# Clears and early weight tiles on another DMA queue, tables ahead of the loop, later tiles behind a gather

## The chip, the cores and the metric

The kernel runs on one core of a Trainium2 chip. Its engines are TensorE (PE, with its weight loads as PEld), VectorE (DVE), ScalarE (ACT), GpSimd (POOL) and SyncE (SP, which issues DMAs). All times are microseconds on the device; less is better. One execution was profiled; the times beside it are of executions without a profile.

## The reference

Causal block attention over 8 batches of 8 heads (576 positions, 64 wide, blocks of 64), then a mixture of 8 experts in which each token goes to its best expert and each expert keeps its 80 tokens with the highest gate:

```python
scores = scale * np.matmul(q, k.transpose(0, 1, 3, 2))
scores = np.where(block_i >= block_j, scores, -1000000000.0)
attn = np.exp(scores - np.max(scores, axis=-1, keepdims=True))
attn = attn / (np.sum(attn, axis=-1, keepdims=True) + 1e-09)
x = np.matmul(attn, v)                     # then (B * S, H * D) = (4608, 512)
...
logits = x @ w_gate                        # (4608, 8)
expert_idx = np.argmax(logits, axis=1)
gate_w = softmax(logits)[arange, expert_idx]
out = zeros((4608, 512))
for e in range(8):
    tok_idx = np.where(expert_idx == e)[0]         # the 80 with the highest gate_w of these
    h = np.maximum(x[tok_idx] @ w1[e], 0.0)        # w1[e]: 512 x 1024
    out[tok_idx] = gate_w[tok_idx, None] * (h @ w2[e])
```

Every row of `out` that no expert writes is zero.

## The kernel before, in words

**Attention.** 32 pairs of heads (4 pairs a batch) run through a software pipeline: turn `i` of the loop at the end of `tile_attn_moe` does, in an order written out in the table `TURN`, the load of pair `i+3` (`load`: four DMAs for q, four for k, into one of three buffers each, lines L392 before and L394 after), the transposes of pair `i+1` (`prep`, DVE, L406 / L409, the q one followed by a scale on POOL, L409 / L412), the scores, maxima and exponentials of pair `i` and the transposes and products with v of pair `i-1`. The Tile framework keeps this order on each engine. The loop starts at `i = -3`. SP issues all loads in order; DVE runs `prep` in order with the maxima of the scores, so a q that has not landed holds up DVE, and PE after it.

**Beside the loop.** Zeros are written to `out` by 18 DMAs of 512 KB (`clear`, L150), in most turns from 4 on, out of a tile `zero`. Three weight tiles of 2 MB (`weights`, L233 / L235; tiles 0 to 2 of 16, the list alternates between w1 and w2) are loaded in turns 8, 16 and 24: the "early tiles". After each batch its rows, their sums and the gate logits are made; `store` writes them to `xs` in DRAM. Tables that the selection uses are made by `constants` (POOL, in turn 3) and `constants2` (DVE and POOL, in turn 5). In `constants2` DVE's table `iota_c16` (L212) needs POOL's `iota_c` (L210), the last of a row of POOL instructions that starts with a copy (L198) of DVE's `sameE` (L195).

**Selection and experts.** After the last store the kernel picks the tokens of each expert (the indices `gi`), POOL gathers each expert's 80 rows from `xs` (L735 / L738, `fetches`), DVE divides them by their sums (`xn`, L824), PE transposes two experts' rows ahead and then multiplies by w1 and w2 (L835 / L840) expert by expert; POOL scatters the result to `out` (L872). The 13 later tiles are issued by SP: two after the last store, a third after `gi`, three more after the fourth gather (`fetches[HOLD]`), the rest one by one between the experts as buffers come free.

Of the kernel before, what the change touches and what calls it, by code (L numbers as in the profile page):

```python
# [18 lines left out]
P = 128  # L19
BLK = 64  # L20
NT = 5
FW0, FWA, FWC, FWB = 3, 3, 1, 2
# [56 lines left out]
def tile_attn_moe(ctx, tc, q, k, v, w_gate, w1, w2, capacity, out, xs=None, dbg=None):  # L79
    nc = tc.nc  # L80
# [41 lines left out]
    for i in range(4):  # L122
        r = slice(32 * i, 32 * i + 32)
# [18 lines left out]
    zero = pb.tile([P, 2 * DM], F32, name="zero")  # L142
    rows = 2 * P
    ov = out.rearrange("(n p r) d -> n p r d", p=P, r=2) if NTOK % rows == 0 else None
    nz = NTOK // rows

    def clear(i):
        if ov is not None:
            if 0 <= i < nz:
                nc.sync.dma_start(ov[i], zero.rearrange("p (r d) -> p r d", r=2))  # L150
        elif i == 0:
            for j in range(NTOK // BLK):
                nc.sync.dma_start(out[j * BLK:(j + 1) * BLK, :], zero[0:BLK, 0:DM])
# [39 lines left out]
    def constants2():  # L193

        nc.vector.tensor_reduce(sameE, ident.rearrange("p (e j) -> p e j", j=16), axis=AX.X, op=ALU.add)  # L195
        nc.gpsimd.memset(sameR3, 0.0)
        nc.vector.tensor_reduce(sameR, ident.rearrange("p (e j) -> p j e", j=16), axis=AX.X, op=ALU.add)
        nc.gpsimd.tensor_copy(same.rearrange("p (e j) -> p e j", j=16), sameE.unsqueeze(2).broadcast_to([P, E, 16]))  # L198
        nc.gpsimd.memset(ones, 1.0)
        nc.gpsimd.iota(iota_s, pattern=[[1, CHUNK]], base=0, channel_multiplier=0,  # L200
                       allow_small_or_imprecise_dtypes=True)
        nc.gpsimd.iota(iota_p, pattern=[[0, 1]], base=0, channel_multiplier=1, allow_small_or_imprecise_dtypes=True)

        nc.gpsimd.affine_select(out=before, in_=same, compare_op=ALU.is_gt, fill=0.0, base=0,
                                pattern=[[1, P]], channel_multiplier=-1)
        nc.gpsimd.affine_select(out=after, in_=same, compare_op=ALU.is_gt, fill=0.0, base=0,
                                pattern=[[-1, P]], channel_multiplier=1)
        nc.gpsimd.tensor_tensor(before1, before, ident, op=ALU.add)
        nc.gpsimd.tensor_tensor(after1, after, ident, op=ALU.add)
        nc.gpsimd.iota(iota_c, pattern=[[1, 16]], base=0, channel_multiplier=0,  # L210
                       allow_small_or_imprecise_dtypes=True)
        nc.vector.tensor_tensor(iota_c16, sameR, iota_c, op=ALU.mult)  # L212
        nc.vector.tensor_reduce(iota_r, iota_c16, axis=AX.X, op=ALU.add)

        nc.gpsimd.tensor_copy(cf, ci)
        nc.vector.scalar_tensor_tensor(cap, cf[:, 1:2], 4294967296.0, cf[:, 0:1], op0=ALU.mult, op1=ALU.add)
        nc.vector.tensor_tensor(caplt, iota_p, cap, op=ALU.is_lt)

    nw = 0
# [5 lines left out]
    def weights(n, after=None):  # L225

        nonlocal nw
        for _ in range(n):
            src, e = wlist[nw]
            w_ = wpools[nw % len(wpools)].tile([P, KP * F], F32, name="w")  # L230
            nw += 1
            wt_[src is w2, e] = w_ = w_.rearrange("p (a f) -> p a f", f=src.shape[2])
            load = nc.sync.dma_start(w_, src[e].rearrange("(a p) f -> p a f", p=P))  # L233
            if after is not None:
                tc.add_manual_dep(load.ins, after.name, mybir.DependencyInfo(  # L235
                    mybir.DependencyClass.Sync, mybir.DependencyReason.DATA))
# [136 lines left out]
    class Pair:  # L373
# [10 lines left out]
        def load(self):  # L384

            b, h0 = self.b, self.h0
            self.nat = [ld.tile([P, S // 32, 32], F32, name=f"ld{x}") for x in range(2)]
            for x in range(2):
                for h in range(2):
                    for i in range(2):  # L390
                        r = slice(h * D + 32 * i, h * D + 32 * i + 32)
                        nc.sync.dma_start(self.nat[x][r], (q, k)[x][b, h0 + h, :, 32 * i:32 * i + 32]  # L392
                                          .rearrange("(g r) d -> r g d", r=32))

        def load_v(self):
# [160 lines left out]
    def step():  # L556
        if todo:
            f, *args = todo.pop(0)
            f(*args)

    with tc.manual_schedule():
        warm(WARM[0], ps_m.tile([P, 512], F32, name="pm"))
        for i in range(-3, n + 2):
            if i == -1:
                nc.sync.dma_start(ci, capacity.bitcast(U32).partition_broadcast(P))
                for h in range(2):
                    nc.sync.dma_start(wgd[h * D:(h + 1) * D, :, h * E:(h + 1) * E], wg_v[h])

            if i >= 4 and (i % 2 or i % 8 == 4) and i < n:
                clear(cleared)  # L570
                cleared += 1
            if i == 3:
                constants()
            if i == 5:
                constants2()
            if i in range(n // 4, n // 4 + 8 * FW0, 8):
                weights(1)
            for d, what, *args in TURN:
                if what == "step":
                    step()  # L580
                elif 0 <= i + d < n and not (what == "flip" and i + d >= n - NP):
                    getattr(pairs[i + d], what)(*args)
            if n - NP <= i - 1 < n:
                pairs[i - 1].flip()
            if i >= 2 and (i - 2) % NP == NP - 1 and i - 2 < n - 1:
                bt = batches[(i - 2) // NP]
                todo += [(bt.recip,), (bt.store,), (bt.logits, 0), (bt.logits, 1), (bt.logits2, 0), (bt.logits2, 1), (bt.gate,),
                         (bt.turn, nc.gpsimd)] + [(bt.turn2,)]
        while cleared < nz:
            clear(cleared)  # L590
            cleared += 1
        while todo:
            step()
        bt = batches[B - 1]
        bt.recip()
        bt.store()
        bt.logits(0)
        bt.logits(1)
        bt.logits2(0, (3, NT))
        bt.logits2(1, (3, NT))  # L600
        bt.gate()
        bt.turn(nc.vector, 2)
        bt.turn2()
# [17 lines left out]
    fwa = late.enter_context(tc.tile_pool(name="fwa", bufs=FWA, **right, **tw))  # L621
    wpools += [fwa] * FWA
    with tc.issue_after(bt.stored.ins):
        weights(2)
    sel2 = late.enter_context(tc.tile_pool(name="sel2", bufs=1, **right, **tw))


# [95 lines left out]
    with nc.allow_low_precision(reason="whole numbers"):  # L723
        vec.tensor_reduce(gi, pick[0:CHUNK, 0:2 * E].rearrange("s (k e) -> s e k", k=2), axis=AX.X, op=ALU.add)

    weights(FWA - 2)
    att2.close()
    fx = late.enter_context(tc.tile_pool(name="fx", bufs=1, **tw))

    xg, fetches = [], []  # L730
# [82 lines left out]
    fwc = late.enter_context(tc.tile_pool(name="fwc", bufs=FWC, **right, **tw))  # L813
    fwb = late.enter_context(tc.tile_pool(name="fwb", bufs=FWB, **tw))
    wpools += [fwc] * FWC + [fwb] * FWB
    weights(FWC + FWB, fetches[HOLD])

    def divide(dst, src):
# [271 lines left out]
```

## Time and profile before

| | |
|---|---|
| times of three executions | 462.54, 463.0, 466.62 us (median 463.0) |
| the profiled execution | 462.94 us, span 460.7 us, mean granted PE clock 0.97 |
| busy time in the span | PE 415.8, PEld 294.5, DVE 284.1, ACT 271.8, POOL 54.1 us |
| DMA | 84.42 MB, 183 GB/s over the span |
| issues from SP | 256 of q and k (72 KB), 18 clears (512 KB, median 5.1 us to landing), 16 weight tiles (2048 KB, 20.6 us) |
| issues from POOL | 8 gathers (7.9 us to landing), 8 scatters (2.9 us) |

How it is read: the loop over the pairs ends at about 330 us, the selection runs to about 345, the experts from there to the end. A row of the timeline gives start, duration, engine, line, operation and `out<-in`; a bracket says how long the engine stood idle before it and what ended that. "SPq" rows are the time in which SP issues DMAs, not that of the transfer. A row of the windows gives the stretch, its length, the busy time of PE, PEld, DVE, ACT and POOL with their instructions, the granted PE clock, the mean busy share of the DMA engines and GB/s.

### The profile page before, as it was taken

How to read it: one execution, taken by the hardware profiler on the slowest of the kernel's cores; microseconds unless marked ns; L12 is line 12 of the kernel's file. 1: busy time of each engine (PE TensorE's matmuls, PEld its weight loads, DVE VectorE, ACT ScalarE, POOL GpSimd, SP SyncE). 2: the span in 40 equal slices, each digit the busy share in tenths (PEclk: the TensorE clock that was granted, in tenths of full speed). 3: DMA queues.
4: the chain of work that ended last, by engine and by line, in shares of the span. 5: the costliest groups of instructions: out<-in, count | busy, mean ns of one | idle time of the engine just before them, and what ended most of it. 6: DMA issues, size and time to landing. Idle time of an engine off the chain costs nothing. (4 is left out here: it accounts for less than half of the span.)

```text
span 460.7 us, 15580 instructions
## 1 busy us (share of the span) xinstructions
PE 415.8 (90%) x6427; PEld 294.5 (64%) x6427; DVE 284.1 (62%) x564; ACT 271.8 (59%) x863; POOL 54.1 (12%) x112
## 2 busy tenths in 40 slices
PE   6899989999999999998999869999866978888992
PEld 3566656666666666566666546666654977888981
DVE  4667778888797796977877567986671221111111
ACT  1788868798788878877887648888420110110000
POOL 2010211010010010101001000100027100000010
PEclk9999989999999999999999979999996899999998
DMA  7577777898787689779769886977089999994000
GB/s 118 103 138 127 176 146 145 186 246 139 166 164 164 125 182 243 166 144 206 150 119 190 236 170 127 190 183 165 3 229 326 332 395 399 394 396 173 19 25 26
DMA packets 230684, 84.42 MB, mean 183 GB/s; under 512 B 196877, under 2 KB 215309, under 8 KB 230608
## 3 DMA queue, kind: packets, MB, share of 16 engines
q1 hardware_dynamic: 229584, 80.93, 72.4%
q0 software_dynamic: 1024, 2.43, 1.8%
q8 instruction: 52, 0.85, 0.8%
q14 instruction: 24, 0.20, 0.1%
HBM read 63.21 MB, written 20.33 MB: 181 GB/s over the span
## 5 line engine op out<-in xcount | busy, mean ns | idle before, releaser
L453 ACT ACTIVATE P<-sc,negm 128x128 f32<-128x128 f32 (+3 forms) x256 | 133.3, 531 | 32.0 <-DVE negm L445 30.1
L445 DVE TENSOR_REDUCE negm<-sc 128x2 f32<-128x1024 f32 (+3 forms) x128 | 100.2, 810 | 34.6 <-PE sc L431 34.2
L424 PE MATMUL sc<-T,T 64*128 64x128 f32 (+3 forms) x512 | 96.1, 475 | 11.6 <-ACT P L453 10.7
L489 PEld LDWEIGHTS pm<-ident,P 64*128 64x128 f32 x1536 | 57.6, 142 | 33.9 <-ACT P L458 9.7
L489 PE MATMUL pm<-ident,P 64*128 64x64 f32 x1536 | 70.0, 231 | 1.7 <-DVE prod L308 0.4
L424 PEld LDWEIGHTS sc<-T,T 64*128 64x128 f32 x512 | 43.2, 193 | 33.5 <-ACT P L453 14.1
L519 PE MATMUL pm<-PT,vn 128*64 128x128 f32 (+1 forms) x512 | 60.7, 379 | 0.0
L406 DVE STREAM_TRANSPOSE T<-ld 128x576 f32<-128x576 f32 x64 | 48.8, 763 | 16.5 <-DMA ld<-in_q_dram 15.1
L453 ACT ACTIVATION_READ_ACCUMULATOR P<-sc,negm 128x1 f32 x256 | 52.7, 206 | 0.0
L409 POOL TENSOR_SCALAR T<-T 128x576 f32<-128x576 f32 x32 | 21.6, 673 | 247.9 <-DVE T L406 189.2
L519 PE MATMUL pm<-PF,vn 128*64 128x64 f32 (+1 forms) x768 | 48.7, 249 | 0.9 <-ACT PF L529 0.9
L519 PEld LDWEIGHTS pm<-PT,vn 128*64 128x64 f32 x512 | 33.5, 137 | 22.9 <-issue 22.9
L835 PE MATMUL ps<-xsT,w 128*64 128x80 f32 x1024 | 41.3, 241 | 4.4 <-issue 4.3
L531 DVE COPY PT<-pm 128x512 f32<-128x512 f32 x64 | 43.5, 680 | 1.1 <-PE pm L489 1.1
L529 ACT COPY PF<-pm 128x512 f32<-128x512 f32 x64 | 34.4, 589 | 15.5 <-PE pm L489 15.5
L835 PEld LDWEIGHTS ps<-xsT,w 128*64 128x64 f32 x1024 | 39.2, 144 | 5.7 <-issue 5.2
L835 PE MATMUL av<-hT,w 128*64 128x80 f32 x1024 | 38.5, 234 | 4.6 <-issue 4.6
L440 PE MATMUL sc<-T,T 64*64 64x288 f32 x256 | 40.9, 441 | 0.4 <-ACT P L453 0.4
L835 PEld LDWEIGHTS av<-hT,w 128*64 128x64 f32 x1024 | 36.6, 137 | 6.7 <-issue 6.7
L529 ACT COPY PT<-pm 128x512 f32<-128x512 f32 x64 | 37.8, 591 | 0.0
L519 PEld LDWEIGHTS pm<-PF,vn 128*64 128x64 f32 x768 | 32.4, 139 | 7.5 <-ACT PF L529 1.1
L458 ACT ACTIVATE P<-sc,negm 128x576 f32<-128x576 f32 x32 | 23.7, 741 | 22.2 <-DVE negm L449 21.9
(164 smaller groups left out, 363.0 us busy)
## 6 DMA issues: line engine op xcount, KB each, us to landing
w<-in_moe_w_dram SPq DMA_DIRECT2D x16, 2048.0 KB, 20.6
ld<-in_q_dram SPq DMA_DIRECT2D x128, 72.0 KB, 3.2
ld<-in_k_dram SPq DMA_DIRECT2D x128, 72.0 KB, 2.7
out_dram<-zero SPq DMA_DIRECT2D x18, 512.0 KB, 5.1
xs<-Y SPq DMA_DIRECT2D x32, 288.0 KB, 4.8
vn<-in_v_dram SPq DMA_DIRECT2D x64, 128.0 KB, 2.9
vt<-in_v_dram SPq DMA_DIRECT2D x32, 32.0 KB, 2.6
xs<-rs SPq DMA_DIRECT2D x8, 16.0 KB, 2.1
```

The lines of the kernel that those rows point to most:

```text
L406: nc.vector.transpose(t, self.nat[x].rearrange("p g d -> p (g d)"))
L409: nc.gpsimd.tensor_scalar(t, t, scalar1=SCALE, scalar2=1.0, op0=ALU.mult, op1=ALU.mult)
L424: nc.tensor.matmul(s[:, h, c:c + P * (u + 1)], lhsT=self.T[0][r, P * u:P * (u + 1)], rhs=self.T[1][r, 0:P * (u + 1)], start=(x == 0), stop ...
L440: nc.tensor.matmul(s[r, c, 0:288], lhsT=self.T[0][r, 512:S], rhs=self.T[1][r, 288 * c:288 * (c + 1)], start=True, stop=True)
L445: nc.vector.tensor_reduce(self.negm[:, u], self.s[g][:, :, c:c + P * (u + 1)], axis=AX.X, op=ALU.max, negate=True)
L453: nc.scalar.activation(Pt[self.i % 2][u][:, h], self.s[g][:, h, c:c + P * (u + 1)], AF.Exp, bias=self.negm[:, u, h:h + 1], scale=1.0, accu ...
L458: nc.scalar.activation(Pt[self.i % 2][4][:, 0:S].rearrange("p (c k) -> p c k", c=2), self.s["4"][:, :, 0:288], AF.Exp, bias=self.negm[:, 4 ...
L489: nc.tensor.transpose(pt[c][:, n_ * BLK:(n_ + 1) * BLK], from_[r, P * j:P * (j + 1)], ident[r, r])
L519: nc.tensor.matmul(to, lhsT=lhs, rhs=rhs, start=(n_ == 0), stop=(n_ == len(steps) - 1))
L529: nc.scalar.copy(*self.out.pop((what, x)))
L531: nc.vector.tensor_copy(*self.out.pop((what, x)))
L835: yield nc.tensor.matmul(dst(b)[64 * c:64 * (c + 1)], lhsT=w_[:, a, col:col + 64], rhs=x_[:, a], start=(a == 0), stop=(a == n - 1))
```

## The change

Four things move; nothing else is computed.

```diff
     def clear(i):
...
-                nc.sync.dma_start(ov[i], zero.rearrange("p (r d) -> p r d", r=2))
+                nc.gpsimd.dma_start(ov[i], zero.rearrange("p (r d) -> p r d", r=2))
...
     def constants2():
...
         nc.vector.tensor_tensor(iota_c16, sameR, iota_c, op=ALU.mult)
         nc.vector.tensor_reduce(iota_r, iota_c16, axis=AX.X, op=ALU.add)
 
+    def constants3():
+
         nc.gpsimd.tensor_copy(cf, ci)
         nc.vector.scalar_tensor_tensor(cap, cf[:, 1:2], 4294967296.0, cf[:, 0:1], op0=ALU.mult, op1=ALU.add)
         nc.vector.tensor_tensor(caplt, iota_p, cap, op=ALU.is_lt)
...
     def weights(n, after=None):
...
-            load = nc.sync.dma_start(w_, src[e].rearrange("(a p) f -> p a f", p=P))
+            load = (nc.gpsimd if nw <= FW0 else nc.sync).dma_start(w_, src[e].rearrange("(a p) f -> p a f", p=P))
...
         def load(self):
...
-                        nc.sync.dma_start(self.nat[x][r], (q, k)[x][b, h0 + h, :, 32 * i:32 * i + 32]
+                        (nc.scalar if x == 1 and self.i == 0 else nc.sync).dma_start(
+                            self.nat[x][r], (q, k)[x][b, h0 + h, :, 32 * i:32 * i + 32]
                                           .rearrange("(g r) d -> r g d", r=32))
...
-            if i == 3:
+            if i == -2:
                 constants()
-            if i == 5:
                 constants2()
+            if i == 1:
+                constants3()
...
     with tc.issue_after(bt.stored.ins):
-        weights(2)
+        weights(1)
...
-    weights(FWA - 2)
...
+    weights(FWA - 1, fetches[0])
     weights(FWC + FWB, fetches[HOLD])
```

`FW0` and `FWA` are 3. `weights(n, after)` makes a tile's DMA wait for `after` to be complete.

Where the instructions go. First DVE at the start of the program: its last set-up instruction, then the transposes of the first two pairs (`T` from `ld`) and the maxima of the first scores. Before:

```order
L124 TENSOR_TENSOR ident<-ramp 32x32 x4
L126 CAST identr<-ident 128x128
L406 STREAM_TRANSPOSE T_205<-ld_168 128x576
L406 STREAM_TRANSPOSE T_212<-ld_169 128x576
L406 STREAM_TRANSPOSE T_231<-ld_178 128x576
L445 TENSOR_REDUCE negm<-sc 128x2 x3
```

And now:

```order
L124 TENSOR_TENSOR ident<-ramp 32x32 x4
L126 CAST identr<-ident 128x128
L195 TENSOR_REDUCE sameE<-ident 128x8
L197 TENSOR_REDUCE sameR_106<-ident 128x16
L212 TENSOR_TENSOR iota_c_117<-sameR_106,iota_c 128x16
L213 TENSOR_REDUCE iota_r<-iota_c_117 128x1
L409 STREAM_TRANSPOSE T_225<-ld_168 128x576
L409 STREAM_TRANSPOSE T_232<-ld_169 128x576
L409 STREAM_TRANSPOSE T_251<-ld_198 128x576
L448 TENSOR_REDUCE negm<-sc 128x2 x3
```

Four instructions of the tables, one of which (L212) waits for POOL, stand ahead of the first transpose.

Then SP's queue after the first store (`xs`), turns 7 to 9, with the loads of q, k and v. Before:

```order
L280 DMA xs<-Y 32x18x128 x4
L150 DMA out_dram<-zero 128x1024
L392 DMA ld_1247<-in_q_dram 32x18x32 x4
L392 DMA ld_1248<-in_k_dram 32x18x32 x4
L399 DMA vn<-in_v_dram 128x4x64 x2
L401 DMA vt_134<-in_v_dram 64x2x64
L233 DMA w<-in_moe_w_dram 128x4x1024
L392 DMA ld_1413<-in_q_dram 32x18x32 x4
```

And now:

```order
L282 DMA xs<-Y 32x18x128 x4
L394 DMA ld_1247<-in_q_dram 32x18x32 x4
L394 DMA ld_1248<-in_k_dram 32x18x32 x4
L402 DMA vn<-in_v_dram 128x4x64 x2
L404 DMA vt_134<-in_v_dram 64x2x64
L394 DMA ld_1413<-in_q_dram 32x18x32 x4
```

On POOL's queue, which held only the scale of each pair's q (`T`) and small work there, these turns now read:

```order
L412 TENSOR_SCALAR T_1093<-T_1093 128x576
L150 DMA out_dram<-zero 128x1024
L412 TENSOR_SCALAR T_1258<-T_1258 128x576
L235 DMA w<-in_moe_w_dram 128x4x1024
L263 MEMSET sums 64x8
L412 TENSOR_SCALAR T_1430<-T_1430 128x576
L349 TENSOR_TENSOR sp<-Gm,sameE 128x320
L150 DMA out_dram<-zero 128x1024
```

The clear and the tile have left the place between the store and the loads and stand between POOL's scales, where nothing of the loop's loads is behind them.

Last, SP's queue after the last store, with the later tiles by number and the end of each row naming what it waits for (the engine whose reading frees the buffer, or a counter of a DMA queue: DMASW is POOL's, DMASW5 here the first gather's). Before:

```order
L233 DMA w_5474<-in_moe_w1_dram 128x4x1024 [waits DMAHW0_49,PE_49]
L233 DMA w_5476<-in_moe_w2_dram 128x8x512 [waits DMAHW1_49,PE_49,Activation_49]
L233 DMA w_5576<-in_moe_w1_dram 128x4x1024 [waits DMAHW2_49]
L233 DMA w_5659<-in_moe_w2_dram 128x8x512 [waits DMAHW3_49,DMASW3_49,Pool_49]
L233 DMA w_5661<-in_moe_w1_dram 128x4x1024 [waits DMAHW4_49]
L233 DMA w_5663<-in_moe_w2_dram 128x8x512 [waits DVE_49,DMAHW5_49,PE_49,Activation_49]
L233 DMA w_5754<-in_moe_w1_dram 128x4x1024 [waits DMAHW6_49,PE_49]
```

And now:

```order
L235 DMA w_5474<-in_moe_w1_dram 128x4x1024 [waits DMAHW3_49,PE_49]
L235 DMA w_5655<-in_moe_w2_dram 128x8x512 [waits DMASW5_49,DMAHW4_49,PE_49,Activation_49]
L235 DMA w_5657<-in_moe_w1_dram 128x4x1024 [waits DMASW4_49,DMASW3_49,DMASW6_49,DMASW2_49,DMASW7_49,DMASW1_49,DMAHW5_49,DMASW0_49,Pool_49]
L235 DMA w_5754<-in_moe_w1_dram 128x4x1024 [waits DMAHW6_49,PE_49]
L235 DMA w_5659<-in_moe_w2_dram 128x8x512 [waits DMAHW7_49,DMASW0_49,Pool_49]
L235 DMA w_5661<-in_moe_w1_dram 128x4x1024 [waits DMAHW0_49]
L235 DMA w_5663<-in_moe_w2_dram 128x8x512 [waits DMAHW1_49,DVE_49,Activation_49]
```

The second tile now waits for the first gather, the third for counters of POOL's queue, and the tile `w_5754`, whose buffer the first expert frees, has moved from the seventh place to the fourth.

## The prediction

> **What bounds the kernel now.** I read the page first, then the share of each engine, then turn by turn where an idle time ends.
>
> ```profile
> span 460.7 us, 15580 instructions
> PE 415.8 (90%) x6427; PEld 294.5 (64%) x6427; DVE 284.1 (62%) x564; ACT 271.8 (59%) x863; POOL 54.1 (12%) x112
> L406 DVE STREAM_TRANSPOSE T<-ld 128x576 f32<-128x576 f32 x64 | 48.8, 763 | 16.5 <-DMA ld<-in_q_dram 15.1
> ```
>
> PE is the busiest engine, but 45 us of the span are not its own. The row of L406 names a candidate: DVE stood 15.1 us in front of transposes whose q had not landed. One POOL instruction, L409, runs once per pair, so its starts are a clock of the loop; I ask the timeline of POOL for them. The first number is the start, the second the length; the bracket is POOL's idle time before.
>
> ```profile
> 20.37 0.67 POOL L409 TENSOR_SCALAR T<-T 128x576 f32<-128x576 f32 x1 [9.47 <-DVE T L406]
> 47.57 0.67 POOL L409 TENSOR_SCALAR T<-T 128x576 f32<-128x576 f32 x1 [8.20 <-DVE T L406]
> 77.83 0.67 POOL L409 TENSOR_SCALAR T<-T 128x576 f32<-128x576 f32 x1 [8.02 <-ACT PT L529]
> 89.16 0.68 POOL L409 TENSOR_SCALAR T<-T 128x576 f32<-128x576 f32 x1 [10.50 <-DVE T L406]
> 127.41 0.67 POOL L409 TENSOR_SCALAR T<-T 128x576 f32<-128x576 f32 x1 [10.86 <-DVE T L406]
> 164.94 0.67 POOL L409 TENSOR_SCALAR T<-T 128x576 f32<-128x576 f32 x1 [10.49 <-DVE T L406]
> ...
> 289.30 0.67 POOL L409 TENSOR_SCALAR T<-T 128x576 f32<-128x576 f32 x1 [10.48 <-DVE T L406]
> ```
>
> From 89.16 to 127.41, and from there to 164.94, are four turns each (one batch): 38.25 and 37.53 us. The next twelve turns end at 289.30: 124.36 us, or 41.5 for four. Equal work, unequal time. The windows of the shortest and the longest block say what the short one is bound by.
>
> ```profile
> 127.40:165.00 37.60, 37.46 (x529) 24.27 (x527) 31.53 (x58) 31.88 (x104) 3.65 (x7) 1.00 0.78 156
> 242.80:289.30 46.50, 40.39 (x533) 25.84 (x531) 32.00 (x58) 32.16 (x105) 3.60 (x6) 0.93 0.84 181
> ```
>
> The columns are window, its length, busy time of PE, PEld, DVE, ACT, POOL, granted PE clock, DMA share, GB/s. In the short block PE is busy for 37.46 of 37.60 us: 37.53 us is what PE needs for four turns. The long block holds the same DVE work (58 instructions, 32.0 us), 6 us without PE, and a lower clock after it. Whatever a block takes above 37.53 is a wait: 0.72 in the first block and 124.36 - 3 x 37.53 = 11.77 in the last three, **12.5 us**. The timelines of DVE and SP name it.
>
> ```profile
> 213.62 0.78 DVE L406 STREAM_TRANSPOSE T<-ld 128x576 f32<-128x576 f32 x1 [2.27 <-DMA ld<-in_q_dram]
> 266.75 0.78 DVE L406 STREAM_TRANSPOSE T<-ld 128x576 f32<-128x576 f32 x1 [5.61 <-DMA ld<-in_q_dram]
> 64.50 2.16 SPq L392 DMA_DIRECT2D ld<-in_q_dram  x4
> 205.08 1.70 SPq L150 DMA_DIRECT2D out_dram<-zero  x1
> 206.83 3.97 SPq L392 DMA_DIRECT2D ld<-in_q_dram  x4
> 254.39 0.59 SPq L233 DMA_DIRECT2D w<-in_moe_w_dram  x1
> 255.08 8.93 SPq L392 DMA_DIRECT2D ld<-in_q_dram  x4
> ```
>
> Four q loads cost SP 2.16 us when nothing stands before them, 3.97 behind a clear of `zero`, and 8.93 behind an early weight tile; the transposes that wait (213.62 and 266.75) read just those loads. SP issues in order, so whatever slows an issue makes every later load late.
>
> **The change, part by part.** *Clears and early tiles leave SP.* SP loses 18 clears and 3 tiles, and what stood behind them. At 205 it gains 1.70 for the clear and up to 3.97 - 2.16 = 1.8 for the loads behind it, 3.5 in all against a wait of 2.27; at 254 it gains 0.59 + 6.77 = 7.4, against 5.61, and has not come in late. So the waits can all go: 12.5 us. The other end is no gain at all, if the bytes and not the queue held the loads back (a rival below); how a load fares beside a tile of another queue no row shows. I take **11 us**, near the upper end, since the rows of SP are issue times and these go. POOL takes the 21 issues over. Their nearest row is the gather:
>
> ```profile
> L735 POOL DMA_INDIRECT xg<-xs,gi x8 | 8.0, 1002 | 6.7 <-ACT occ L779 4.6 <-issue 2.1
> ```
>
> 80 rows cost 1.0 us. By rows, as an estimate, a clear (128) costs 1.6 us and a tile 6 to 13 (512 or 1024 rows); by instruction each costs 1.0. Ahead of its next L409 POOL idles 8.0 to 10.9 us in the rows above, so both ends are hidden but for the third tile, which could hold one L409 back by some 4 us. I cost it at nothing; without the cover every microsecond over counts once per clear.
>
> *Selection's tables leave turn 5.* There DVE stood for POOL's last table, in front of the transpose of the next pair:
>
> ```profile
> 58.13 0.18 DVE L212 TENSOR_TENSOR iota_c<-sameR,iota_c 128x16 f32<-128x16 f32 x1 [1.94 <-POOL iota_c L210]
> 58.79 0.78 DVE L406 STREAM_TRANSPOSE T<-ld 128x576 f32<-128x576 f32 x1
> ```
>
> What the wait and the instructions around it cost is read from L409. The three turns with them took 77.83 - 47.57 = 30.26 us, three before them 47.57 - 20.37 = 27.20: 3.06. `constants3` returns two DVE instructions of 0.3 us in all, whose input POOL has made long before, at turn 1. I take **3 us**.
>
> *The start.* The tables now stand ahead of the first transposes, and DVE waits there for POOL's last table instead.
>
> ```profile
> 4.88 0.78 DVE L406 STREAM_TRANSPOSE T<-ld 128x576 f32<-128x576 f32 x1 [1.68 <-DMA ld<-in_q_dram]
> 7.10 0.78 DVE L406 STREAM_TRANSPOSE T<-ld 128x576 f32<-128x576 f32 x1 [1.44 <-DMA ld<-in_k_dram]
> 1.76 0.21 POOL L551 MEMSET wgd<- 128x128 f32 x1
> 30.20 0.96 POOL L185 MEMSET zero<- 128x1024 f32 x1
> 55.99 0.29 POOL L198 COPY same<-sameE 128x128 f32<-128x128 f32 x1 [7.66 <-DVE sameE L195]
> 57.96 0.14 POOL L210 IOTA iota_c<- 128x16 f32 x1
> ```
>
> POOL is free at 1.97; `constants` (0.96 for `zero`, some 0.8 for the rest) ends near 3.7, and L198 to L210 took 57.96 + 0.14 - 55.99 = 2.1: `iota_c` is there at 5.8. DVE needs 58.79 - 58.13 = 0.66 at most from L212 on, so q is transposed at 6.3 to 6.5, not 4.88. k, issued by ACT beside q, has landed by then, so its transpose follows at 7.0 to 7.2, where it stood at 7.10. What ACT saves is spent on the wait. I take **0** (+0.2 to -1.5 if POOL is slower beside DVE).
>
> *Later tiles behind the gather.* The first late tile (`w_5474`) still follows the last store; the second and third (`w_5655`, `w_5657`) now wait for the first gather, and so do all tiles behind them on SP; the fourth in SP's row, `w_5754`, now stands ahead of three others and waits until the first expert's L835 block has read an early tile.
>
> ```profile
> 337.51 8.57 SPq L233 DMA_DIRECT2D w<-in_moe_w_dram  x3
> 345.99 1.22 POOL L735 DMA_INDIRECT xg<-xs,gi  x1 [4.56 <-ACT occ L779]
> 347.51 0.97 POOL L735 DMA_INDIRECT xg<-xs,gi  x1 [0.30 <-issue]
> 353.28 0.76 DVE L824 TENSOR_TENSOR xn<-xg 80x256 f32<-80x256 f32 x2 [8.23 <-DMA xg<-xs,gi]
> 354.37 0.76 DVE L824 TENSOR_TENSOR xn<-xg 80x256 f32<-80x256 f32 x2 [0.33 <-DMA xg<-xs,gi]
> 355.90 7.03 PE L835 MATMUL ps<-xsT,w 128*64 128x80 f32 x128
> out_dram<-y,si POOLq DMA_INDIRECT x8, 2.9
> 397.48 3.12 PE L835 MATMUL av<-hT,w 128*64 128x80 f32 x83 [0.96 <-issue]
> 446.22 4.49 PEld L835 LDWEIGHTS av<-hT,w 128*64 128x64 f32 x128 [0.19 <-issue]
> 362.00:364.00 2.00, 2.00 (x52) 1.82 (x50) 0.60 (x2) 0.84 (x2) 0.00 (x0) 1.00 1.07 343
> DMA  7577777898787689779769886977089999994000
> ```
>
> The gathers took 354.37 - 347.51 = 6.9 us beside three tiles; a scatter of the same 80 rows takes 2.9. The second gather decides, since PE transposes both experts' rows before L835. Landing after 2.9 us it comes at 350.4, after 6.9 (the new tiles start when the first lands) where it was. I take 351: **3.4 us** earlier. Against that, the first late tile alone (2.1 MB at the 343 GB/s of the window at 362) is through by 344, and the engines idle until 349. The DMA line of the page has 40 slices of 11.5 us; its last digit that isn't 0, a 4, is the slice from 415 to 426, so the stream of tiles now ends near 420, and would end near 425, or up to 430 if the third tile waits for the last gather or the fourth for PE with nothing else under way. While it flows PE pays 0.96 us at its gaps, afterwards 0.19; PE being earlier and the stream later, one or two more gaps cost the long price, 1.4 us. The net is **2 us**. No tile is late by this: the last is wanted at 446.22, a few microseconds sooner after the change.
>
> Sum: 11 + 3 + 0 + 2 = 16 us off the profiled execution's 462.94 us (its span is 460.7, the rest lies around it; the median is 463.0): **447 us**.
>
> **A rule on the clock.** The 128 matmuls at 355.90 took 7.03 us, where the last 128 weights took 4.49; at 362 the granted clock is 1.00 again. The Trainium skill ("TensorE: Matmul & The Clock Gate", section "Part 1: The HAM clock gate") says that the clock is halved after an idle window and restored after a busy one, on a window that runs freely. By that rule a shorter idle stretch ahead of L835 could leave it the full clock, up to 2.5 us more; the rows show one such start and it was slow, so the sum counts nothing for it.
>
> **Rivals.**
> - *The engines, not the queue.* The loads share the same engines wherever a tile is issued; then the waits stay, and only turn 5 and the tail gain: 463 - 5 = 458; with half of the waits 453. For it speaks a DMA share of 0.84 in the long block; against it that the block at 127 runs at 0.78 without a wait, and that SP's late issues are what the late loads stand behind. The Trainium skill ("DMA: Bandwidth & Descriptors", section "Issuing engines are not separate DMA queues") speaks for this rival: issuing from several engines saves only the issue time, which it calls usually small. Here the issue time is not small (8.93 against 2.16 us).
> - *POOL's issues become the bound (slower).* Place: between two L409. If a clear holds POOL longer than about 9 us, L409 and the scores behind it come late, each microsecond 18 times: at 11 us, 447 + 18 x 2 = 483. It ends slower from about 10 us. Against it: a gather's 1.0 us is a tenth of that.
> - *The changes do what they say but the start costs what turn 5 gave.* If POOL's tables run twice as long ahead of the loop (two more microseconds) and the second gather lands where it did: 463 - 11 - 1 + 1.4 = 452.
>
> **How the numbers follow.** Forecast 0.68, engines 0.18, POOL 0.05, start and tail lost 0.09. The range runs from 441 (12.5 + 3.1 + 0.2 + 3.4 + 2.5 = 21.7 off, the last for a first block of matmuls as fast as the last one) to 458, the first rival's far end. About 1% (458.4) is what a measurement of this kernel can tell from no change: faster 0.87 (the forecast and the last rival 0.77, the first rival 0.10), same 0.08 (the rest of the first), slower 0.05.
>
> **What would show it.** Right: L409 about 37.5 us apart per four turns throughout; no q wait over 1 us; SP's q loads at about 2.2 us everywhere; DVE held at L212 until about 6; L835 starting 3 us sooner after the gather's issue. Wrong: waits on q that remain with SP free, POOL's issues of 8 us and more, or PE waiting for tiles in the tail.

## The result and the profile after

| | before | changed |
|---|---|---|
| median of the runs beside each other | 463.56 us | 452.48 us (fastest 448.28) |
| the same, timed again later | 464.33 us | 450.78 us (fastest 450.29) |
| ratio of times, 95% interval | | 0.969 [0.963, 0.975]; again 0.970 [0.966, 0.974] |
| profiled execution, its span | 462.94, 460.7 | 452.48, 450.4; again 450.48, 448.4 |

The change makes the kernel about 3.1% faster. The forecast was 447 us in a range from 441 to 458. The single executions of the changed kernel lie further apart than those of before: of its eleven, seven took 448 to 453 us, three 457 to 459 and one 2126, and the ratios are of the seven (the mean of the ten without the last is 452.6 us, against 464.5 before, 2.6% less).

The page of the changed kernel, its span, two engines and the transposes:

```profile
span 450.4 us, 15586 instructions
PE 408.7 (91%) x6427; PEld 290.0 (64%) x6427; DVE 283.6 (63%) x564; ACT 271.6 (60%) x863; POOL 65.7 (15%) x133
L409 DVE STREAM_TRANSPOSE T<-ld 128x576 f32<-128x576 f32 x64 | 48.7, 762 | 4.1 <-DMA ld<-in_q_dram 4.1
```

DVE's wait for q and k went from 16.5 us to 4.1. POOL has 21 instructions more, the issues it took over. The clock of the loop is POOL's scaling again (L412 now), in the timeline of the changed kernel:

```profile
47.37 0.67 POOL L412 TENSOR_SCALAR T<-T 128x576 f32<-128x576 f32 x1 [7.52 <-DVE T L409]
...
74.39 0.66 POOL L412 TENSOR_SCALAR T<-T 128x576 f32<-128x576 f32 x1 [7.83 <-DVE T L409]
85.70 0.67 POOL L412 TENSOR_SCALAR T<-T 128x576 f32<-128x576 f32 x1 [9.74 <-DVE T L409]
...
123.59 0.66 POOL L412 TENSOR_SCALAR T<-T 128x576 f32<-128x576 f32 x1 [9.98 <-DVE T L409]
...
237.22 0.67 POOL L412 TENSOR_SCALAR T<-T 128x576 f32<-128x576 f32 x1 [9.58 <-DVE T L409]
...
278.23 0.66 POOL L412 TENSOR_SCALAR T<-T 128x576 f32<-128x576 f32 x1 [9.98 <-DVE T L409]
```

From 85.70 to 123.59 are four turns: 37.89 us. The next three blocks end at 237.22 and take 37.88 each on average; the last takes 41.01. The three turns from 47.37 to 74.39 took 27.02 us, against 30.26 before. In the last block one wait is left. The timelines of POOL, SP and DVE around it:

```profile
226.53 0.96 POOL L235 DMA_DIRECT2D w<-in_moe_w_dram  x1
228.94 1.29 SPq L279 DMA_DIRECT2D xs<-rs  x1
230.29 3.92 SPq L280 DMA_DIRECT2D xs<-rs  x1
234.26 5.21 SPq L282 DMA_DIRECT2D xs<-Y  x4
239.52 4.17 SPq L394 DMA_DIRECT2D ld<-in_q_dram  x4
247.73 0.78 DVE L409 STREAM_TRANSPOSE T<-ld 128x576 f32<-128x576 f32 x1 [2.69 <-DMA ld<-in_q_dram]
```

The third early tile starts on POOL's queue at 226.53. SP, though it no longer issues it, needs 10.4 us for the six issues of the batch's store that follow (5.1 us in an undisturbed one), and the q loads behind the store are late by 2.69 us.

The tail, in the timelines of POOL, DVE and PE, and then the windows of the ten and sixty microseconds from the first expert's first matmul on (before, then changed; columns as in the prediction's windows):

```profile
334.71 1.11 POOL L738 DMA_INDIRECT xg<-xs,gi  x1 [4.34 <-ACT occ L782]
339.44 2.17 DVE L829 TENSOR_TENSOR xn<-xg 80x256 f32<-80x256 f32 x6 [5.62 <-DMA xg<-xs,gi]
341.35 6.98 PE L840 MATMUL ps<-xsT,w 128*64 128x80 f32 x148
```

```profile
355.90:365.90 10.00, 10.00 (x208) 9.82 (x208) 2.97 (x13) 1.83 (x5) 2.73 (x9) 0.75 1.03 314
365.90:425.90 60.00, 51.04 (x1268) 47.56 (x1265) 9.04 (x28) 6.16 (x16) 3.75 (x4) 1.00 0.94 354
```

```profile
341.35:351.35 10.00, 9.50 (x210) 9.16 (x208) 2.14 (x12) 2.16 (x5) 4.97 (x11) 0.83 1.00 300
351.35:411.35 60.00, 48.91 (x1220) 45.69 (x1222) 8.65 (x27) 5.81 (x14) 3.75 (x4) 1.00 1.02 389
```

The matmuls start 6.64 us after the first gather's issue, against 9.91 before: 3.27 gained. In the sixty microseconds that follow the DMA engines now work through (1.02 against 0.94) and PE is busy for 2.1 us less.

The last difference lies behind the last scatter, where the program closes. The row of POOL's DRAIN in the source view, before and changed (shortest, median and longest of three, in ns, then the first and the last start in us):

```profile
L1085 POOLq DRAIN  x3: 46/98/1383, 458.4 to 460.4; - x3
```

```profile
L1090 POOLq DRAIN  x3: 46/104/3098, 446.4 to 450.1; - x3
```

The longest DRAIN takes 1.7 us longer. The whole difference by stretches, from the marks above and those of the prediction; "again" is the second profiled execution of the changed kernel, whose marks follow the table:

| stretch (us) | before | changed | again | forecast of the change |
|---|---|---|---|---|
| start to the sixth scaling | 47.57 | 47.37 | 46.21 | 0 |
| three turns, with turn 5 | 30.26 | 27.02 | 27.03 | -3 |
| one turn | 11.33 | 11.31 | 11.31 | |
| five blocks of four turns | 200.14 | 192.53 | 189.45 | -11 |
| to the first gather | 56.69 | 56.48 | 57.08 | |
| gather to first expert matmul | 9.91 | 6.64 | 6.71 | -3.4 |
| first expert matmul to last scatter | 97.26 | 99.14 | 100.76 | +1.4 |
| last scatter to the end | 7.54 | 9.91 | 9.85 | 0 |
| sum | 460.7 | 450.4 | 448.4 | -16 |

```profile
46.21 0.67 POOL L412 TENSOR_SCALAR T<-T 128x576 f32<-128x576 f32 x1 [7.52 <-DVE T L409]
...
84.55 0.67 POOL L412 TENSOR_SCALAR T<-T 128x576 f32<-128x576 f32 x1 [9.74 <-DVE T L409]
...
274.00 0.66 POOL L412 TENSOR_SCALAR T<-T 128x576 f32<-128x576 f32 x1 [9.98 <-DVE T L409]
```

### The profile page after: what moved, and what is told of

It is laid out like the page before. It is cut to its first block, busy times and chain, and to the rows that moved or that the text cites. A ratio compares the mean times of both kernels' runs of the same rounds, so it can differ in the third digit from the quotient of the medians.

```text
span 450.4 us, 15586 instructions
## 1 busy us (share of the span) xinstructions
PE 408.7 (91%) x6427; PEld 290.0 (64%) x6427; DVE 283.6 (63%) x564; ACT 271.6 (60%) x863; POOL 65.7 (15%) x133
## 5 line engine op out<-in xcount | busy, mean ns | idle before, releaser
L427 PE MATMUL sc<-T,T 64*128 64x128 f32 (+3 forms) x512 | 94.0, 466 | 5.0 <-ACT P L456 3.5
L427 PEld LDWEIGHTS sc<-T,T 64*128 64x128 f32 x512 | 42.2, 190 | 25.9 <-ACT P L456 6.7
L412 POOL TENSOR_SCALAR T<-T 128x576 f32<-128x576 f32 x32 | 21.3, 666 | 230.3 <-DVE T L409 215.0
```

Source lines behind the costliest of these rows:

```text
L412: nc.gpsimd.tensor_scalar(t, t, scalar1=SCALE, scalar2=1.0, op0=ALU.mult, op1=ALU.mult)
L427: nc.tensor.matmul(s[:, h, c:c + P * (u + 1)], lhsT=self.T[0][r, P * u:P * (u + 1)], rhs=self.T[1][r, 0:P * (u + 1)], start=(x == 0), stop ...
```

## Experiments

Theory: a clear or a tile in SP's row delays the loads behind it there, so that moving the issue is enough (queue). Rival: the bytes hold the loads back whoever issues them (engines). The first four runs do one part of the change each; the kernel before, run beside them, had a median of 465.28 us. The gains given are worked out from the ratios; the bare medians would make them up to 1.4 us larger (3.0 us for the clears).

**Clears alone.**

```
-                nc.sync.dma_start(ov[i], zero.rearrange("p (r d) -> p r d", r=2))
+                nc.gpsimd.dma_start(ov[i], zero.rearrange("p (r d) -> p r d", r=2))
```

> The kernel before with one edit: the 18 clears of zero are issued by POOL; tiles, tables and later tiles stay. In the loop of before the turns from 89.16 to 289.30 us took 10.7 us more than undisturbed turns; some 6 of these stand behind the early tile at 254.39, some 4.7 behind clears. Queue theory (a clear delays the loads behind it in SP's row): the 4.7 go, 463.5 - 4.7 = about 459, the waits on q that are left stand behind tiles only. Engines theory (the bytes of the clear hold the loads back, whoever issues them): no change, 463.5. Cost theory (POOL's issues delay its own work): each issue takes 0.6 us and lies in POOL's idle time, so nothing; if it does not, up to 18 x 0.6 = 11 us slower.

Measured: 462.25 us, ratio 0.996 [0.993, 0.9996], so 1.7 us. The timelines of SP and DVE:

```profile
201.11 4.04 SPq L280 DMA_DIRECT2D xs<-Y  x4
205.19 5.04 SPq L392 DMA_DIRECT2D ld<-in_q_dram  x4
213.17 0.78 DVE L406 STREAM_TRANSPOSE T<-ld 128x576 f32<-128x576 f32 x1 [2.63 <-DMA ld<-in_q_dram]
```

This is the prediction's own example, the wait of 2.27 us at 213.62. The clear is gone from between store and load, and the wait is still there: the loads behind a store take 5.04 us without a clear too (3.97 before). The 3.5 us that the prediction gave to the clear at this place did not come. Nor did SP come much sooner: from its first store to its sixth 12 clears (12.7 us, summed over their rows) are gone, but the 160 loads of q and k there took 134.3 us in place of 125.5 and those of v 37.3 in place of 35.3. It reached the sixth store 210.0 us after the first, against 211.2 before. POOL's issues cost nothing in the loop: undisturbed turns take 8.64, 8.91 and 9.02 us, as before.

**Early tiles alone.**

```
-            load = nc.sync.dma_start(w_, src[e].rearrange("(a p) f -> p a f", p=P))
+            load = (nc.gpsimd if nw <= FW0 else nc.sync).dma_start(w_, src[e].rearrange("(a p) f -> p a f", p=P))
```

> The kernel before with one edit: the 3 early weight tiles are issued by POOL; the clears stay on SP. Queue theory: the 6 us behind the tile at 254.39 go, 463.5 - 6 = about 457.5, and the four loads behind it are issued in about 2.2 us. Engines theory: the 2.1 MB of the tile still hold the loads back, 463.5 and a wait on q of 3 to 6 us where it was.

Measured: 465.89 us, ratio 1.003 [1.0001, 1.006]. The timelines of POOL, SP and DVE:

```profile
232.54 0.96 POOL L233 DMA_DIRECT2D w<-in_moe_w_dram  x1
234.71 9.80 SPq L392 DMA_DIRECT2D ld<-in_k_dram  x4
260.15 0.78 DVE L406 STREAM_TRANSPOSE T<-ld 128x576 f32<-128x576 f32 x1 [6.26 <-DMA ld<-in_q_dram]
```

Nothing of the tile is in SP's row, and SP's four k loads still take 9.80 us while it flows. For a tile moved alone the engines rival holds: the wait is still there, 6.26 us where it had been 5.61, though POOL issued the tile 22 us earlier than SP had (232.54 against 254.39).

**Tables alone.**

```
-            if i == 3:
+            if i == -2:
                 constants()
-            if i == 5:
                 constants2()
+            if i == 1:
+                constants3()
```

(and k of the first pair by ACT)

> The kernel before with one part of the change: the tables ahead of the loop (constants and constants2 at turn -2, constants3 at turn 1) and the first pair's k issued by ACT. Theory of the prediction: turn 5 gives 3.0 to 3.2 us, the start costs nothing: 463.5 - 3 = about 460.5, first L409-type scaling on POOL at about 7.8 us in place of 5.75, but the third scaling at 20.4 or sooner. Rival: the loop is held elsewhere (by SP's loads) a little later, so that turn 5's 3 us are waited off at the next late load: 462 to 463.5.

Measured: 462.54 us, ratio 0.997 [0.994, 0.9995], 1.5 us. Turn 5 gave its 3.2 us (its three turns took 27.02), but the last scaling came at 306.62 in place of 307.51: the block from the eighteenth to the twenty-second scaling took 41.57 us where it had taken 38.58. At the start the first scaling stood at 7.72, as expected, the third at 20.75, a little late. The rival is what happened: most of the time was waited off at the next late load.

**Later tiles alone.**

```
     with tc.issue_after(bt.stored.ins):
-        weights(2)
+        weights(1)
...
-    weights(FWA - 2)
...
+    weights(FWA - 1, fetches[0])
     weights(FWC + FWB, fetches[HOLD])
```

> The kernel before with one part of the change: the second and third late tile wait for the first gather, in a row before the others. Theory of the prediction: the first expert's matmuls start 3.3 us sooner after the first gather's issue, 1.4 us are given back by gaps of PE in the tail: 463.5 - 2 = 461.5. Rival: the gaps take more than the start gives, since the stream of tiles then sets the pace of the tail: 463.5 to 465.

Measured: 460.54 us, ratio 0.991 [0.988, 0.994], 4.1 us. Its windows, five microseconds ahead of the first expert matmul and ten behind it:

```profile
345.46:350.46 5.00, 4.24 (x15) 2.95 (x13) 0.90 (x3) 0.43 (x1) 3.93 (x4) 0.66 0.56 150
350.46:360.46 10.00, 9.23 (x231) 8.71 (x233) 3.35 (x15) 2.17 (x5) 5.79 (x12) 1.00 1.00 295
```

The first matmul stands 5.17 us behind the gather's issue, and here the block runs at the full clock: 231 matmuls in ten microseconds against 208. From the gather to the last scatter are 104.33 us, against 107.17 before.

The four ratios multiply to 0.987, or 6 us; the whole change gave 14. The parts need each other, and the next four runs ask which.

**Early tiles back on SP, clears on POOL.** The tile's line of the change undone.

> The changed kernel with one part undone: the three early tiles are issued by SP again, in the same turns (8, 16, 24); clears stay on POOL. Moved alone, the tiles cost 1.3 us (ratio 1.0029), with waits on q of 2.72 and 6.26 us beside the third tile. Theory that the bytes of a tile hold the loads back whoever issues it: the time stays within 2 us of the changed kernel, 448 to 452, perhaps a little faster. Queue theory (with clears off SP the tile is what is left in front of the loads): 454 to 457, and a wait on q of 4 us or more behind the third tile.

Measured: 458.75 us, ratio 0.988 [0.984, 0.991], 8 us slower than the changed kernel. The wait is the one that the queue theory forecast, the time is above it. Here the queue does count, as the timelines of SP and DVE behind the third tile show:

```profile
248.81 8.16 SPq L394 DMA_DIRECT2D ld<-in_q_dram  x4
260.23 0.78 DVE L409 STREAM_TRANSPOSE T<-ld 128x576 f32<-128x576 f32 x1 [5.07 <-DMA ld<-in_q_dram]
```

The q loads behind the tile take 8.16 us, and DVE waits 5.07 us for them. How much of the 8 us this queue is worth is less sure: the last run below was as slow with the changed kernel's own loop.

**Clears back on SP, tiles on POOL.** The clear's line undone.

> The changed kernel with one part undone: the 18 clears are issued by SP again; tiles stay on POOL. Moved alone the clears gave 1.7 us. If the parts add up, this takes 2 us more than the changed kernel, 451 to 453. If the waits are a threshold (SP is late only when clear, store and tile come together, and each part alone leaves it late), it takes 6 to 9 us more, 455 to 459, most of it in the turns around the third tile.

Measured: 462.93 us, ratio 0.996 [0.993, 0.9995]: 12 us of the gain are gone, more than either theory forecast. The timelines of POOL, SP and DVE around the third tile:

```profile
232.88 0.96 POOL L235 DMA_DIRECT2D w<-in_moe_w_dram  x1
235.19 10.28 SPq L402 DMA_DIRECT2D vn<-in_v_dram  x2
247.46 0.54 SPq L279 DMA_DIRECT2D xs<-rs  x1
261.35 0.78 DVE L409 STREAM_TRANSPOSE T<-ld 128x576 f32<-128x576 f32 x1 [9.94 <-DMA ld<-in_q_dram]
```

With the clears in its row SP reaches the store 14.6 us after the tile's issue, in the changed kernel 2.4. What meets the tile is then the turn's loads, the store comes after, and the next q loads behind both. The clears need not be the whole cause: the last run below shows the same order of events with the clears on POOL.

**Tiles two turns sooner, on POOL, and then on SP.**

```
-            if i in range(n // 4, n // 4 + 8 * FW0, 8):
+            if i in range(n // 4 - 2, n // 4 - 2 + 8 * FW0, 8):
```

> The changed kernel with the three early tiles two turns sooner (6, 14, 22 in place of 8, 16, 24), on POOL. In the changed kernel the third tile is issued at 226.53, 4 us ahead of the store of a batch, whose issues then take 10.4 us in place of 5.1, and q is waited for 2.69 us at 247.73. Theory: with the tile through before the store there is no wait on q left in the loop, each four turns 37.88 us apart: 3 us off the profiled 452.5, and the spread of the runs (448.3 to 452.5) closes at its lower end, 448. Rival: the tile meets plain loads two turns sooner and holds them back by as much: 450 to 453.

> As the kernel with the tiles two turns sooner, but these three issued by SP: it parts the place of a tile from its queue. If the place decides (a tile next to a store is what makes loads late), this is as fast as with POOL, 447 to 449. If the queue decides, the loads behind each tile take 7 to 9 us to issue and a wait on q of 1 us or more stays: 451 to 455.

Measured: 459.27 us (0.990 [0.986, 0.994]) and 459.65 us (0.990 [0.986, 0.994]). My expectation was wrong, its rival too low: in these executions the place next to the store was the better one. Away from it the tile meets plain loads. The timelines of POOL, SP and DVE of the first of the two:

```profile
210.03 0.96 POOL L235 DMA_DIRECT2D w<-in_moe_w_dram  x1
212.58 9.70 SPq L394 DMA_DIRECT2D ld<-in_k_dram  x4
222.13 0.78 DVE L409 STREAM_TRANSPOSE T<-ld 128x576 f32<-128x576 f32 x1 [5.60 <-DMA ld<-in_q_dram]
```

On SP the four q loads behind the third tile took 10.18 us; the waits were 3.72 and 4.86 us, neither of them on these loads but both behind the next store, which SP reached late. The two times are the same, so at this place the queue makes no measurable difference.

**The changed kernel again.** No edit.

> The changed kernel as it is, timed again beside the three others. The first five executions gave 448.3, 448.6, 452.5 and 458.4 (one more was disturbed). The two kernels that differ from it only in the early tiles gave 458 to 460. Theory that the place of a tile against a store decides, and that this place shifts by a few microseconds from execution to execution: 447 to 459, in the profiled one a wait on q where a tile meets a store, none else. Rival (the kernel is steady and the 5 first executions were lucky): 456 to 460 throughout.

Measured: 450.78 us, ratio 0.970 [0.966, 0.974]. The third tile and what it met, in the timelines of POOL, SP and DVE:

```profile
225.41 0.96 POOL L235 DMA_DIRECT2D w<-in_moe_w_dram  x1
230.80 6.16 SPq L282 DMA_DIRECT2D xs<-Y  x4
244.50 0.78 DVE L409 STREAM_TRANSPOSE T<-ld 128x576 f32<-128x576 f32 x1 [0.57 <-DMA ld<-in_q_dram]
```

SP was 2.3 us further on against the loop's clock, and the same program waits 0.57 us where it had waited 2.69. All five blocks took 37.89.

**Early tiles in quarters.**

```
+                s_ = src[e].rearrange("(a p) f -> p a f", p=P)
+                g = s_.shape[1] // 4
+                pieces.extend((w_[:, g * x:g * x + g], s_[:, g * x:g * x + g]) for x in range(4))
...
+            if i in (2, 3, 6, 8, 10, 14, 16, 18, 22, 24, 26, 30):
+                if not pieces:
+                    weights(1)
+                nc.gpsimd.dma_start(*pieces.pop(0))
```

> The changed kernel with each early tile in four loads of 0.5 MB, one to a turn (turns 2, 3, 6, 8, 10, 14, 16, 18, 22, 24, 26, 30), on POOL like the clears. Moving 18 clears of 0.5 MB to POOL left the turns next to them undisturbed (8.63 to 9.03 us), a tile of 2.1 MB did not. Theory that a burst of 2.1 MB is what holds the loads back: no wait on q over 1 us in the loop, blocks of 37.9 us throughout, last scaling on POOL at 293 to 294 in place of 296.42; nine more POOL loads make the final DRAIN 0.7 us longer; 447 to 449 in every execution. Rival (the sum of the bytes decides): waits as before, spread over more turns, 450 to 459.

Measured: 456.73 us, ratio 0.980 [0.975, 0.985]. The time is the rival's, and so are the waits in the profiled execution (459.98 us). Only one group of four loads of SP was held for over 6 us (6.46, behind the first store), but SP lost its lead bit by bit, reached the third batch's store later than in the changed kernel (159.25 against 152.75), and q was waited for 4.08 us at 172.08. The DRAIN took 3833 ns, which is 3098 + 9 x 81.7, the 0.7 us forecast.

**Clears in eight pieces.**

```
+                z_ = zero.rearrange("p (r d) -> p r d", r=2)
+                for x in range(0, P, P // 8):
+                    nc.gpsimd.dma_start(ov[i, x:x + P // 8], z_[x:x + P // 8])
```

> The changed kernel with each clear in 8 pieces of 64 KB: 126 more loads on POOL, the same bytes. It prices what was costed at nothing. In the loop: 8 issues of 0.6 us are 4.8 us of the 8 to 10 us that POOL idles per turn: no change if hidden; where a turn is not, L412 comes late. At the end: POOL's last DRAIN took 1383 ns in the kernel before (16 loads by POOL, the gathers and scatters), 1628 with 3 more, 2853 with 18 more and 3098 with 21 more, 81.7 ns for each; so here 3.10 + 126 x 0.0817 = 13.4 us, and the time is 10 us longer than the changed kernel's. If the DRAIN only waits for transfers under way, it stays near 3 us and the time is the same.

Measured: 450.21 us, ratio 0.969 [0.966, 0.972], the changed kernel's time. The groups of lines, then the timelines of POOL and SP around the third tile:

```profile
L152 POOL DMA_DIRECT2D out_dram<-zero x144 | 70.6, 500 | 2.6 <-issue 2.6
```

```profile
226.47 0.98 POOL L237 DMA_DIRECT2D w<-in_moe_w_dram  x1
227.97 7.25 SPq L284 DMA_DIRECT2D xs<-Y  x4
```

In the loop the cover holds: 144 issues, 60 us more of POOL's time, and turns of 8.65, 8.90 and 9.03 us as ever. At the end my rule failed: the DRAIN took 3507 ns, not 13.4 us. Up to 46 DMAs issued by POOL the 81.7 ns each hold (1383, 1628, 2853, 3098, 3833 ns for 16, 19, 34, 37 and 46); at 163 they don't. What caps it no run here tells. This run also has the tile that meets the store fully (its four large issues begin 1.5 us behind the tile's), and no wait on q in the loop after the start.

**Later tiles back.** The later tiles' lines undone in the changed kernel.

> The changed kernel with one part undone: the second and third late tile follow the last store again, ahead of the first gather. Theory of the prediction: first expert matmul 9.9 us after the gather's issue in place of 6.6, 1.4 us fewer gaps later; 2 us slower than the changed kernel. Rival (the tail is bound by the stream of tiles and PE's gaps beside it, so that an earlier start is waited off): from the gather to PE's end 106 to 107 us as in the kernels without this part, against 104.7 in the profiled changed kernel and 106.0 to 106.6 in four relatives of it; 0 to 1 us slower.

Measured: 460.51 us, ratio 0.983 [0.977, 0.989]. Both forecasts, 2 us and 0 to 1 us slower, were missed, and the time says nothing of the tail: up to the last store this program is the changed kernel's, and in its profiled execution (462.33 us) DVE waited 8.91 us for q behind the third tile. The timelines of POOL, SP and DVE:

```profile
226.69 0.97 POOL L235 DMA_DIRECT2D w<-in_moe_w_dram  x1
230.61 7.29 SPq L402 DMA_DIRECT2D vn<-in_v_dram  x2
241.50 4.06 SPq L282 DMA_DIRECT2D xs<-Y  x4
254.12 0.78 DVE L409 STREAM_TRANSPOSE T<-ld 128x576 f32<-128x576 f32 x1 [8.91 <-DMA ld<-in_q_dram]
```

POOL issues the tile at the same point of the loop as in the changed kernel (226.53), but SP is 2 us further back (its k loads there start at 226.99 against 224.98), so the tile meets loads of v and not the store, as with the clears back on SP. The store comes 7.2 us later (241.50 against 234.26), and the wait is 6.2 us longer. The tail itself: first matmul 10.47 us after the gather, last scatter 97.58 us later, 108.05 in all against 105.78 and 107.47 in the two profiles of the changed kernel. So the later tiles' part is worth 0.6 to 2.3 us by these rows. Over all profiles, the stretch from the gather to the last scatter takes 104.3 to 107.7 us in the nine with this part (mean 106.8) and 107.2 to 108.4 in the five without it (107.8): about 1 us. Why all six executions (453.1 to 462.3 us) were slower than the changed kernel's median, with the same loop, is open. It limits what the times of the other runs can say of the loop's parts: a difference of 8 us came here without any edit to the loop, so for these parts the rows of the profiles count for more than the times.

## Why the prediction was right, and where it was not

**Loads, clears, tiles (11 us).** The size was right: 7.6 us in the first profile, 10.7 in the second. The floor was misread: 37.53 us, the short block from 127.41, began with a scaling 0.36 us late (its turns took 11.69 and then 8.27; undisturbed ones 11.32 and 8.63). A block takes 37.88, and what could be gained was 200.14 - 5 x 37.88 = 10.7, not 12.5. That 11 came out so near is partly luck: 12.5 was 1.8 too much, and 1.5 of it was not taken for another reason.

The reason was only half right. "SP issues in order, so whatever slows an issue makes every later load late" holds. The step that failed is the next one, that the slow issues go when clears and tiles leave SP. An issue on SP is slow while other bytes flow, whoever sent them (9.80 us for four loads beside a tile of POOL's). So SP's q loads did not become 2.2 us everywhere: in the changed kernel they take 4 to 5 us behind a store, and 9.46 us behind the first store, beside the first tile of POOL's queue, where nothing waited for them.

What the change bought is SP's lead. One batch is four scalings, so the stores from the second to the sixth have as their marks the 13th, 17th, 21st, 25th and 29th scaling. The start of SP's store (`xs<-Y`) against this mark, from the timelines of six profiles, puts the lead in numbers:

| kernel | store behind its mark (us) | wait on q behind it (us) |
|---|---|---|
| before, fourth and fifth store | 8.80, 8.84 | 2.27, 2.43 |
| clears alone, fourth and sixth | 9.71, 9.25 | 2.63, 1.92 |
| changed, fifth (beside the tile) | 8.35 | 2.69 |
| again, fifth (beside the tile) | 6.01 | 0.57 |
| later tiles back, fifth (behind the tile) | 15.43 | 8.91 |
| changed, second to fourth and sixth | 2.60 to 5.43 | none |
| clears in eight pieces, second to sixth | 1.47 to 4.17 | none |

The fourteen profiles have seventy such stores. Of the 40 that SP starts up to 6.51 us behind the mark, one is followed by a wait, of 0.57 us; the loads behind the others are in time, even at 4 to 5 us. Of the 12 from 7.02 to 8.43 us, seven are followed by waits of 0.65 to 2.69 us, so the edge isn't sharp. All 18 from 8.49 us on are followed by one, of 1.86 to 9.94 us, as a rule the longer the later the store. The transpose that waits begins 11.7 to 13.7 us after the store's start each time. Changed, again and later tiles back are one program up to the last store, so between their three rows no edit of the loop stands.

SP's own pace closes the account. Five batches cost the loop 189.4 us without a wait (5 x 37.88). From its first store to its sixth SP took 211.15 us before and 200.39 in the changed kernel, 21.75 and 10.99 more. Before, 11.00 of this came out of the lead (the first store stood 4.59 us ahead of the ninth scaling, the sixth 6.41 behind the 29th) and 10.75 were waits between these scalings; changed, 7.87 and 3.12.

A tile ahead of loads takes some 7 us of the lead (0.59 + 8.16 - 2.16 = 6.6; before 0.59 + 8.93 - 2.16 = 7.4). A clear's issue takes 0.6 to 1.7 us of SP's row, but with the clears alone gone SP gained only 1.2 us in five batches. With one part undone the longest wait was 5.07 or 9.94 us; with neither undone it was 0.57, 2.69 or, in the later tiles back, 8.91. So the parts needn't add, since a part shows only when the lead is used up. This rests on rows side by side: no edit moved the store by itself, how much each part is worth is not shown, and what puts SP further on in one execution of a program than in another is open.

**The engines rival** was given 458 us and 0.18. Its mechanism was shown for tiles: their bytes hold loads up whoever issues them. The Trainium skill ("DMA: Bandwidth & Descriptors", section "Issuing engines are not separate DMA queues") says that transfers share the DMA engines whoever starts them, and the tile moved alone agrees (1.003). Its other half, that only the usually small issue time is saved, is not all that this case shows: with the clears off SP, tiles on its queue brought back the wait of 5.07 us, and the time was 8 us longer.

**POOL's issues.** Costed at nothing, and nothing it was, in the loop. The estimates by rows were far too high: a clear's issue took 0.60 us and a tile's 0.86 (estimated at 1.6 and 6 to 13 by rows, at 1.0 by instruction), so an issue's cost hardly grows with what it moves. The slower rival (an issue of over 9 us) is out. What the sum lacked, put at nothing without a reason, is the end: 2.4 us, of them 1.7 in POOL's DRAIN. The stretch behind the last scatter goes with the number of DMAs that POOL issued: 7.5 us at 16 of them, 9.2 to 9.3 at 34, 9.9 at 37, 10.7 at 46.

**Tables (3 us)**: 3.24 and 3.23 us, whole; alone, 0.9 us were left at the end of the loop, where late loads took the rest. **The start (0)**: DVE went on at 5.80 as forecast, q was transposed at 6.89, half a microsecond later than said, after a wait of 0.71 us for its load, and the sixth scaling came 0.2 us sooner, in the second profile 1.4. The latter is no gain of the change: the sixth scaling stands between 46.1 and 47.6 us in the profiles with the tables moved and in those without.

**The tail (2 us).** The start of the experts' matmuls was right: 3.27 and 3.20 us sooner, forecast 3.4. What is given back was mis-sized: 1.9 and 3.5 us where 1.4 was taken, so the net is 1.4 in one profile and a loss of 0.3 in the other (about 1 us gained over all profiles). Behind the gather the DMA engines are now full for all of the sixty microseconds (1.02 against 0.94), and PE is busy 2.1 us less in them. The clock's part, not counted, came in the later tiles' own run: 231 matmuls in ten microseconds. There PE had been busy for 4.24 of the 5 us ahead, before for 1.49; in the changed kernel, with 2.5 of 5 us busy, the clock was granted 0.83 in the first ten. The Trainium skill ("TensorE: Matmul & The Clock Gate", section "Part 1: The HAM clock gate") has the clock restored by a busy stretch, and these three rows agree. Other profiles don't follow the busy time in that order: 3.36 of 5 us and 0.53 granted with the sooner tiles on SP, 0.97 and 0.83 with the tiles back on SP. Of the fourteen starts only that one had the full clock.

In sum: 16 forecast, 10.3 and 12.3 measured in the spans. The loop fell short of its 11 by 3.4 and 0.3, the tail of its 2 by 0.6 and 2.3, and the end took 2.4 and 2.3 that were not in the sum; the start gave 0.2 and 1.4 back. No kernel here beats the changed one: the clears in eight pieces take the same time.

## What to carry to other kernels

An engine that issues loads in order has a lead, and a wait shows only when it is used up: measure the lead (issue of a late item against a clock of the loop) before pricing what is taken off, and expect that parts of such a change can be worth little alone. Moving an issue to another queue takes away its place in the row, not its bytes; ask what will stand in the row while they flow, and prefer something that nobody waits for soon, such as a store. Before a block is taken as the floor, compare its turns with those of the others: a mark that came late makes the next block short.

## What the runs showed of the hardware

- POOL's final DRAIN took 1383 ns in programs with 16 DMAs issued by POOL and 81.7 ns more for each further one up to 46, alike for clears of 0.5 MB and tiles of 2 MB; with 163 it took 3507 ns.
- Four loads of 72 KB cost SP 2.16 us to issue, and up to 9.8 us while a 2 MB tile from POOL's queue flowed.
- POOL issued a 512 KB clear in 0.60 us, a 64 KB piece in 0.50 and a 2 MB tile in 0.86.
- One program's wait at one place was 2.69 us in one execution and 0.57 in another, as SP stood 2.3 us further on against the loop; with the same loop and SP 7.1 us further back it was 8.91.
